# The first pass over a batch in two steps of groups instead of three, with two of its scores in the feed-forward's own banks and a pause behind each maximum and each exponential

## The chip, the cores and the metric

The kernel runs on one core of a Trainium2 chip. The metric is the device time of one execution in microseconds (us). Before the change it is 1489.42 us, the median of three runs (1488.94 to 1490.77).

## The reference

Two things are computed one after the other: an attention through 32 inducing points, and a feed-forward layer with a leaky ReLU over its result.

```
x: 4 batches x 12480 tokens x 128;  inducing: 32 x 128
def mab(q, kv):
    s = scale * (q @ kv.T);  s = s - s.max(-1);  a = exp(s);  a /= a.sum(-1) + 1e-9
    return a @ kv
h   = mab(inducing, x)          # per batch: 32 x 128, over all 12480 tokens
y   = mab(x, h)                 # per token, over 32 rows
out = max(0.01 * g, g) @ w_out, with g = y @ w_in      # 128 -> 2048 -> 128, for 49920 tokens
```

So every batch needs a first pass over all its tokens (scores against the inducing points, a maximum, exponentials, and products with the tokens' rows) before `h` is known, and only then the second softmax and the feed-forward work of that batch can begin.

## The kernel before

**Tiles and units.** A batch has 12480 tokens: six groups 0 to 5 of 2048 tokens and a rest group RG (number 6) of 192. The feed-forward work runs over tiles of 512 columns: four tiles per full group, and one tile of 384 columns for the rests of two batches together (the pair tile). There are 98 tiles, and each takes 16 units (one for each 128 of the 2048 hidden columns): 1568 units, numbered u = 16 x tile + f. One unit is four matmuls on TensorE: `ph` (L718, hidden values into one of three PSUM banks), and three `po` (L757: high and low part of the hidden values with high and low part of w_out). ScalarE makes the high part `ghi` from `ph` (L731), VectorE the low part `glo` (L739). TensorE runs three units ahead with `ph` (LOOK = 3): `ph` of unit u+3 is issued, then the three `po` of unit u. Behind the last unit of a tile stands one more product (L776, with `m2s`), which adds the linear part.

**Where the batches stand.** Batch 0 is prepared by a list written out by hand (ORDER). Its tiles 0 to 23 are units 0 to 383. Batch 1 begins with tiles 24 to 27 (its group 0), then comes tile 28, the pair tile of the rests of batches 0 and 1 (units 448 to 463), then group 1 from tile 29. Tile 77 is the pair tile of batches 2 and 3.

**What is woven in.** The loop over units (L1316 to L1341) issues one unit, and after it lets generators make one step each: `stores`, `stacking`, `fetches`, `seconds`, `scores`, `values`. A step that returns HEAVY (15) puts a debt on the loop that is paid off with 4 per unit (5 in batch 0); while there is debt, nothing but `stacking` and `fetches` makes a step. So the order on every engine is written by this loop, and each engine works through its own order.

- `first_scores` (L362) turns a batch's tokens (L397, VectorE) and takes the first pass in the steps of PASSES (L129): [RG, 0, 1], [2, 3], [4, 5]. A step's scores (`s1_ps`, L264, with `indT`) go to TensorE in one stretch, with up to two second scores of the batch before (`s2_ps`, L264, with `hT`) that were waiting, and with the value products of the step before (`h_ps`, L440). `peaks` (L269) takes the maxima on VectorE, `running` (L294) the running maximum and the exponentials.
- `first_values` (L462) turns the exponentials and adds the value products up (`hacc`). Then `expand_weights` (L533) makes the weights `hws` of that batch.
- `second` (L577) makes one group's second softmax and its turned result: `aT` for a full group, `aTr` for the rest group (L623). The groups come in the order 0, 1, RG, 2, 3, 4, 5 (L1341).
- `stack` (L628) splits that into `ahi` (L645, ScalarE) and `alo` (L650, GpSimd), and copies the pieces into the tile `A4` by DMAs on SyncE's queue (L664): four DMAs for a full tile, and 24 for a pair tile (two batches, three pieces, four rows of partitions), because its pieces are 32 partitions x 64 columns.
- `load_rows` (L216) fetches token rows `xr` by DMA on the same queue, `load_blocks` (L243) the blocks `xc` to be turned, `store` (L781) writes results: four DMAs of `osb` per tile.

`ph` of a tile's first unit waits for the DMAs of its `A4`.

Of the kernel before, what the change touches and what calls it, by code (L numbers as in the profile page):

```python
# [20 lines left out]
def induced_attention_then_leaky_ffn(  # L21
# [106 lines left out]
    ring = set()  # L128
    PASSES = [[RG, 0, 1], [2, 3], [4, 5]]  # L129
    PASS_OF = {g: p for p, gs in enumerate(PASSES) for g in gs}  # L130
# [71 lines left out]
    def room(n=1):  # L202

        return not rows_live or rows_made[0] + n - 1 - min(i for i, _ in rows_live) < XR

# [63 lines left out]
    def peaks(b, p, sps):  # L269

        gs = PASSES[p]
        rm = sb.tile([P, len(gs)], F32, tag="rm", name="rm", bufs=2)
        if RG in gs:
            nc.vector.memset(rm[:, :1], -3.0e38)
        for i, g in enumerate(gs):
            _, J, K = GROUPS[g]
            w, rows = 32 * K, 32 * J
            if g == RG:
                e = sb.tile([P, w], F32, tag="er", name="er", bufs=1)
            else:  # L280
                e = sb.tile([P, TOK], F32, tag="e", name="e", bufs=2)
            nc.vector.tensor_scalar(  # L282
                out=e[:rows, :w],
                in0=sps[g][:rows, :w],
                scalar1=1.0,
                scalar2=None,
                op0=ALU.mult,
                op1=ALU.max,
                accum_out=rm[:rows, i : i + 1],
            )  # L290
            ex[b, g] = e
        return rm

    def running(b, p, rm):  # L294
        gs = PASSES[p]
        n = len(gs)
        nm_old = maxima.get(b)
        zg = sb.tile([P, 3], F32, tag="zg", name="zg", bufs=2)
# [3 lines left out]
        four = sb.tile([M, 12], F32, tag="rd", name="four", bufs=2)  # L302
        al = None
# [3 lines left out]
        if nm_old is None:  # L307
            nc.vector.tensor_reduce(out=nm[:M], in_=four[:, : 4 * n], op=ALU.min, axis=AX.X)
        else:
            least = sb.tile([M, 12], F32, tag="least", name="least", bufs=2)  # L310
# [12 lines left out]
        for i, g in enumerate(gs):  # L323
            _, J, K = GROUPS[g]
            w, rows = 32 * K, 32 * J
            e = ex[b, g]
            nc.scalar.activation(  # L327
                e[:rows, :w], e[:rows, :w], AF.Exp, bias=nm[:rows], scale=SCALE,
                accum_out=zg[:rows, i : i + 1],
            )  # L330
            yield
        zs = sb.tile([P, 1], F32, tag="zs", name="zs", bufs=2)
# [29 lines left out]
    def first_scores(b):  # L362


        halves = [(RG, 0, 3)] + [(g, j0, 2) for g in range(RG) for j0 in (0, 2)]
        blocks = {}
# [9 lines left out]
        for p, gs in enumerate(PASSES):  # L376
# [24 lines left out]
            while p and not ((b, p - 1) in ready and landed(b, p - 1)):  # L401
                yield
            while b - 1 not in hw or hw[b - 1][2] is None or not room(min(2, len(waiting))):
# [16 lines left out]
            rm = peaks(b, p, sps)  # L420
            yield HEAVY
# [40 lines left out]
    def first_values(b):  # L462

        hacc = None
        for p, gs in enumerate(PASSES):
            while (b, p) not in summed:
                yield
            for g in gs:
# [5 lines left out]
                else:  # L474
                    ay = sb.tile([P, 16, M], F32, tag="ay", name="ay", bufs=2)
                nc.vector.transpose(ay[:rows, :K, :].rearrange("p k m -> p (k m)"), e[:rows, : 32 * K])
# [30 lines left out]
    def normalise(b, hacc, rz):  # L507

        same = e128.rearrange("p j m -> p (j m)")
        hs = sb.tile([P, C], F32, tag="hs", name="hs", bufs=1)  # L510
        nc.scalar.mul(hs, hacc, rz)
# [21 lines left out]
    def expand_weights(b):  # L533
# [4 lines left out]
        if b:  # L538
            while not room(2):
# [37 lines left out]
    def second(b, g, engines=None):  # L577
# [4 lines left out]
        rows, w = 32 * J, 32 * K  # L582
        if b == B - 1 and (b, g) not in early and g != RG and g > 1:
            while hw[b][2] is None or not room(len(waiting)):
# [257 lines left out]
    def start(stacking, seconds, chosen):  # L842
# [57 lines left out]
        def peak(g):  # L900
# [5 lines left out]
            if g == RG:  # L906
                e = sb.tile([P, TOK], F32, tag="e", name="e", bufs=2)
            else:
                e = sb.tile([P, TOK], F32, tag="A4", name="e0", bufs=A4_BUFS)
# [61 lines left out]
        def Y(g):  # L971
            J, K, rows, w = size(g)
            V["ay", g] = ay = sb.tile([P, 16, M], F32, tag="ay", name="ay", bufs=2)
            nc.vector.transpose(
# [35 lines left out]
        def gather(p):  # L1010
            hp = V.pop(("hp", p))[:, :C]
            if p == len(STEPS) - 1:
                V["hs"] = new = sb.tile([P, C], F32, tag="hs", name="hs", bufs=1)
                nc.vector.scalar_tensor_tensor(
# [20 lines left out]
        def scaled():  # L1035
            V["samez"] = r = sb.tile([P, P], F32, tag="samez", name="samez", bufs=1)
            nc.scalar.mul(r, same, V["rz"])
# [76 lines left out]
        def first_second():  # L1114
# [3 lines left out]
            yield  # L1118
            y = sb.tile([P, 16, M], F32, tag="y", name="y", bufs=1)
            chosen["ysub"].tensor_tensor(  # L1120
# [23 lines left out]
        def scales():  # L1144
            apart = sb.tile([P, 4, 16], F32, tag="apart", name="apart", bufs=1)
            nc.vector.tensor_tensor(
# [10 lines left out]
        def scales_copy():  # L1157
            r = sb.tile([P, 4, 16], F32, tag="scr", name="scr", bufs=1)
            nc.scalar.copy(r.rearrange("p t k -> p (t k)"), V.pop("sc")[:, :64])
# [46 lines left out]
        def second_turned(g):  # L1206
# [3 lines left out]
            if g:  # L1210
                y = sb.tile([P, 16, M], F32, tag="y", name="y", bufs=1)
                nc.vector.transpose(y.rearrange("p k m -> p (k m)"), V.pop(("s2", g)))
# [90 lines left out]
    with tc.manual_schedule():  # L1303
# [12 lines left out]
        for u in range(WOVEN, NT * NF):  # L1316
# [12 lines left out]
            if u >= 52 and u % 2:  # L1329
                step(fetches)  # L1330
            if not debt[0]:
                step(seconds)
            if u >= max(due[0], 52) and not debt[0]:
                due[0] = u + (2 if b or u % 4 else 1)
                step(scores)
            if u >= 52 and (u >= due[1] or hw[max(hw)][2] is None) and not debt[0]:
                due[1] = u + (2 if b or u % 4 else 1)
                known = len(hw)
                step(values)
                if len(hw) > known:  # L1340
                    seconds += [second(known, g) for g in [0, 1, RG, 2, 3, 4, 5]]  # L1341
        for gen in stores:
# [35 lines left out]
```

## Time and profile before

| | |
|---|---|
| median of three runs | 1489.42 us |
| the profiled execution: its time, and the span of its instructions | 1489.34 us, 1487.1 us |
| TensorE (PE) busy | 1477.0 us, 99% |
| VectorE (DVE) busy | 1262.5 us, 85% |
| ScalarE (ACT) busy | 998.8 us, 67% |
| GpSimd (POOL) busy | 116.5 us, 8% |
| share of PE in the chain that ended last | 97% |

Busy time is the time in which at least one instruction of the engine runs. The profiled execution took 2.24 us more than its span: what lies ahead of the first and behind the last instruction. SPq is SyncE's queue of DMA issues; an issue there has a duration of its own, and the data lands later.

### The profile page before, as it was taken

Reading aid. Unit: us, or ns where it says so; the run is one execution under the profiler, and the core shown is the slowest. Engines: PE = TensorE matmul, PEld = TensorE weight load, DVE = VectorE, ACT = ScalarE, POOL = GpSimd, SP = SyncE. Lnnn points to the kernel's source line nnn. Section 1 sums busy time; section 2 is a strip of 40 time slices with the busy share of each in tenths; the row PEclk is TensorE's granted clock in tenths of the full one; section 3 lists DMA queues with packets and bytes.
Section 4 is the critical chain, followed back from the end, with each engine's and each line's share of the span. In section 5 each row is a group of like instructions: output and inputs, shape, how many; then the busy total and the mean of one; then the engine's idle time right before and its main releaser. Section 6 shows DMA issues by size and latency. Waiting matters only on the chain.

```text
span 1487.1 us, 22254 instructions
## 1 busy us (share of the span) xinstructions
PE 1477.0 (99%) x7861; PEld 1260.3 (85%) x7861; DVE 1262.5 (85%) x2129; ACT 998.8 (67%) x1749; POOL 116.5 (8%) x186
## 2 busy tenths in 40 slices
PE   8999999999999999999999999999999999999998
PEld 6788888888888888888888888888888898888887
DVE  6889889889898898889898898788888888888886
ACT  6766767666665766667665766676776666666665
POOL 1320100000100100000100100010100000000000
PEclk9999999999999999999999999999999999999999
DMA  8336255444444342343443441231212212212211
GB/s 287 68 80 124 47 94 113 94 91 77 88 91 89 89 90 52 57 87 70 89 86 69 109 92 17 49 71 21 45 37 39 44 21 51 43 22 50 41 24 22
DMA packets 402079, 105.23 MB, mean 71 GB/s; under 512 B 372624, under 2 KB 375088, under 8 KB 401968
## 3 DMA queue, kind: packets, MB, share of 16 engines
q1 hardware_dynamic: 401920, 103.80, 34.5%
q8 instruction: 62, 1.02, 0.3%
q14 instruction: 49, 0.40, 0.1%
q10 hardware_dynamic: 48, 0.02, 0.0%
HBM read 48.94 MB, written 25.56 MB: 50 GB/s over the span
## 4 chain that ended last, share of the span: by engine, by line
PE 97%; DMA 1%; SPq 0%; ACT 0%; DVE 0%; issue 0%; DVEq 0%
PE po L757 68%; PE ph L718 23%; PE s_ps L264 3%; PE po L776 1%; DMA xr<-in_x_dram 1%; PE h_ps L440 1%; PE h_ps L1001 0%; SPq L852 0%; PE hw_ps L547 0%; PE w_ps L1101 0%; PE winT_ps L1091 0%; ACT ghi L731 0%; PE a_ps L1182 0%; DVE osb L786 0%; ACT e L327 0%
## 5 line engine op out<-in xcount | busy, mean ns | idle before, releaser
L731 ACT ACTIVATE ghi<-ph 128x512 fp32r<-128x512 f32 (+1 forms) x1568 | 928.4, 595 | 460.1 <-PE ph L718 454.0
L739 DVE SCALAR_TENSOR_TENSOR glo<-ph,ghi 128x512 fp32r<-128x512 f32 (+1 forms) x1568 | 1042.9, 680 | 183.3 <-ACT ghi L731 161.6
L718 PE MATMUL ph<-A,hws 128*128 128x512 f32 (+1 forms) x1600 | 595.0, 377 | 0.4 <-ACT A L1186 0.3
L757 PE MATMUL po<-glo,w_hi 128*128 128x512 f32 (+1 forms) x1568 | 593.0, 378 | 0.0
L757 PE MATMUL po<-ghi,w_lo 128*128 128x512 f32 (+1 forms) x1568 | 593.0, 378 | 0.0
L757 PE MATMUL po<-ghi,w_hi 128*128 128x512 f32 (+1 forms) x1568 | 592.8, 379 | 0.0
L718 PEld LDWEIGHTS ph<-A,hws 128*128 128x128 f32 x1600 | 301.8, 189 | 58.1 <-DVE e L282 5.0
L757 PEld LDWEIGHTS po<-glo,w_hi 128*128 128x128 f32 x1568 | 296.4, 189 | 41.2
L757 PEld LDWEIGHTS po<-ghi,w_lo 128*128 128x128 f32 x1568 | 296.3, 189 | 41.2
L757 PEld LDWEIGHTS po<-ghi,w_hi 128*128 128x128 f32 x1568 | 296.4, 189 | 39.9 <-ACT ghi L731 0.2
L786 DVE STREAM_TRANSPOSE osb<-po 128x512 f32<-128x512 f32 (+1 forms) x98 | 68.9, 703 | 1.5 <-PE po L776 1.5
L650 POOL TENSOR_TENSOR alo<-aT,ahi 128x512 fp32r<-128x512 f32 x22 | 28.2, 1282 | 516.9 <-ACT ahi L645 479.7
L397 DVE STREAM_TRANSPOSE xT<-xc 128x512 f32<-128x512 f32 x72 | 50.5, 701 | 0.0
L599 POOL TENSOR_TENSOR y<-y,mx 128x512 f32<-128x512 f32 x23 | 24.2, 1050 | 228.9 <-DVE mx L597 194.5
L614 POOL TENSOR_TENSOR y<-y,sm 128x512 f32<-128x512 f32 x23 | 24.2, 1050 | 199.8 <-DVE sm L612 168.9
L776 PE MATMUL po<-A,m2s 128*128 128x512 f32 (+1 forms) x100 | 37.1, 374 | 0.0
L357 DVE STREAM_TRANSPOSE y<-s_ps 128x512 f32<-128x512 f32 x22 | 15.8, 716 | 10.9 <-PE s_ps L264 9.3
L264 PE MATMUL s_ps<-xT,hT 128*32 128x512 f32 x192 | 23.8, 596 | 0.4 <-ACT hT L1045 0.4
L264 PE MATMUL s_ps<-xT,indT 128*32 128x512 f32 x192 | 24.0, 594 | 0.0
L776 PEld LDWEIGHTS po<-A,m2s 128*128 128x128 f32 x100 | 18.9, 189 | 2.6
L282 DVE TENSOR_SCALAR_CACHE_REDUCE e<-s_ps 128x512 f32<-128x512 f32 x18 | 12.4, 690 | 8.0 <-PE s_ps L264 7.3
L440 PEld LDWEIGHTS h_ps<-xr,ay 128*32 128x32 f32 x576 | 15.2, 110 | 2.9 <-issue 2.6
(165 smaller groups left out, 375.1 us busy)
## 6 DMA issues: line engine op xcount, KB each, us to landing
xr<-in_x_dram SPq DMA_DIRECT2D x96, 256.0 KB, 4.4
out_dram<-osb SPq DMA_DIRECT2D x384, 64.0 KB, 2.2
xc<-in_x_dram SPq DMA_DIRECT2D x288, 64.0 KB, 2.7
A<-ahi SPq DMA_DIRECT2D x188, 64.0 KB, 2.0
A<-alo SPq DMA_DIRECT2D x188, 64.0 KB, 2.0
hws<-hilo SPq DMA_DIRECT2D x64, 64.0 KB, 2.0
raw<-in_moe_w_in_dram SPq DMA_DIRECT2D x4, 512.0 KB, 7.3
raw<-in_moe_w_out_dram SPq DMA_DIRECT2D x4, 512.0 KB, 9.4
```

Of the source, the lines that this page charges most:

```text
L264: nc.tensor.matmul(dst, lhsT, rhs, start=True, stop=True)
L397: nc.vector.transpose(t[:, j, :], blk.rearrange("p n c -> p (n c)"))
L440: nc.tensor.matmul(hp[32 * k : 32 * k + 32, :C], ay[:rows, 4 * q + k, :], xb[:rows, k, :], start=(i == 0 and q == 0), stop=(last[k] == i a ...
L599: engines[0].tensor_tensor(out=yv, in0=yv, in1=mx[:rows, :K].unsqueeze(2).broadcast_to([rows, K, M]), op=ALU.subtract,)
L614: engines[1].tensor_tensor(out=yv, in0=yv, in1=smv.unsqueeze(2).broadcast_to([rows, K, M]), op=ALU.mult)
L650: (engine or nc.gpsimd).tensor_tensor(out=alo[sl], in0=aT.pop((b, g))[: 32 * J, :], in1=ahi[sl].bitcast(F32), op=ALU.subtract,)
L718: nc.tensor.matmul(ph[:, o : o + w], hw[b][1][:, f * P : (f + 1) * P], woven(A4[t][:, o : o + w], t), start=True, stop=True,)
L731: nc.scalar.activation(halves(ghi[:, :n], t)[1], live[u][2], AF.Relu)
L739: nc.vector.scalar_tensor_tensor(out=halves(glo[:, :n], t)[1], in0=ph, scalar=0.0, in1=halves(ghi[:, :n], t)[1].bitcast(F32), op0=ALU.max, ...
L757: nc.tensor.matmul(accs[t][:, :n], w[:, f, :], woven(r[:, :n], t), start=(f == 0 and w is w_hi and r is live[u][0]), stop=False,)
L776: nc.tensor.matmul(accs[t][:, o : o + w], hw[b][2], woven(a4[:, o : o + w], t), start=False, stop=(o + w == n),)
L786: nc.vector.transpose(osb[:, :n], po[:, :n])
```

## The change

The first pass has two steps, [0, 1, 2] and [RG, 5, 3, 4], instead of three. In the first step all waiting second scores (three of them now, groups 3 to 5; groups RG, 2, 0 and 1 are taken in `expand_weights`) go into the three `ph` banks, and the step's own three scores into the two auxiliary banks and the `hp` bank. In the second step RG and 5 go into `ph` banks. Behind each maximum but the last of a step and behind each exponential stands HEAVY. Tokens' rows are taken when a slot is free, not when the oldest is. In the loop `seconds` and `scores` are stepped in that order as before, `values` comes first only while a batch's weights are not finished, and a debt made by one ends the others' turn. Some tiles share a tag (and so a buffer) to make room for a third `e` and a third `ay`.

```
-    PASSES = [[RG, 0, 1], [2, 3], [4, 5]]
+    PASSES = [[0, 1, 2], [RG, 5, 3, 4]]
...
-        return not rows_live or rows_made[0] + n - 1 - min(i for i, _ in rows_live) < XR
+        return len(rows_live) + n <= XR
...
-                e = sb.tile([P, TOK], F32, tag="e", name="e", bufs=2)
+                e = sb.tile([P, TOK], F32, tag="e", name="e", bufs=3)
...
             ex[b, g] = e
+            if i + 1 < len(gs) and g != RG:
+                yield HEAVY
...
                 accum_out=zg[:rows, i : i + 1],
             )
-            yield
+            yield HEAVY
...
-        halves = [(RG, 0, 3)] + [(g, j0, 2) for g in range(RG) for j0 in (0, 2)]
+        halves = [h for gs in PASSES for g in gs for h in ([(RG, 0, 3)] if g == RG else [(g, 0, 2), (g, 2, 2)])]
...
-            for q in [waiting.pop(0) for _ in range(min(2, len(waiting)))]:
+            for q in [waiting.pop(0) for _ in range(len(waiting))]:
...
-                if g == RG:
+                if g == 2:
                     sps[g] = ps_s.tile([P, TOK], F32, tag="hp", name="s1_ps")
+                elif g in (RG, 5):
+                    sps[g] = gen_ps("s1_ps")
                 else:
                     sps[g] = aux_ps("s1_ps")
...
-            for g, ps in [(RG, gen_ps("s2_ps")), (0, aux_ps("s2_ps")), (1, ps_s.tile([P, TOK], F32, tag="hp", name="s2_ps"))]:
+            for g in (RG, 2, 0, 1):
+                if g == 1:
+                    ps = ps_s.tile([P, TOK], F32, tag="hp", name="s2_ps")
+                else:
+                    ps = aux_ps("s2_ps") if g == 0 else gen_ps("s2_ps")
                 second_scores(b, g, ps)
                 turned(b, g, ps)
-            waiting.extend(range(2, RG))
+            waiting.extend(range(3, RG))
...
-            if not debt[0]:
-                step(seconds)
-            if u >= max(due[0], 52) and not debt[0]:
-                due[0] = u + (2 if b or u % 4 else 1)
-                step(scores)
-            if u >= 52 and (u >= due[1] or hw[max(hw)][2] is None) and not debt[0]:
...
+            urgent = hw[max(hw)][2] is None
+            for lane in (values, seconds, scores) if urgent else (seconds, scores, values):
+                if debt[0]:
+                    break
+                if lane is seconds:
+                    step(seconds)
+                elif lane is scores:
+                    if u >= max(due[0], 52):
+                        due[0] = u + (2 if b or u % 4 else 1)
+                        step(scores)
+                elif u >= 52 and (u >= due[1] or urgent):
...
```

**Place one: VectorE, from the first score stretch of batch 2 to the turned rest group `aTr` of batch 1.** Before; `y<-s_ps` are the second scores, `e,rm<-s_ps` the maxima, and each `glo` is one unit:

```order
L357 STREAM_TRANSPOSE y<-s_ps 128x512 x2
L274 MEMSET rm 128x1
L282 TENSOR_SCALAR er,rm<-s_ps 96x64
L282 TENSOR_SCALAR e,rm<-s_ps 128x512 x2
L739 SCALAR_TENSOR_TENSOR glo<-ph,ghi 128x512 x3
L300 MEMSET zg 128x1
L739 SCALAR_TENSOR_TENSOR glo<-ph,ghi 128x512
L623 STREAM_TRANSPOSE aTr<-yr 96x64
```

There `aTr` stands four units behind the stretch. The same place of the kernel after the change, in two pieces that follow each other:

```order
L359 STREAM_TRANSPOSE y<-s_ps 128x512 x3
L282 TENSOR_SCALAR e,rm<-s_ps 128x512
L747 SCALAR_TENSOR_TENSOR glo<-ph,ghi 128x512 x4
L631 STREAM_TRANSPOSE aT<-y 128x512
L747 SCALAR_TENSOR_TENSOR glo<-ph,ghi 128x512 x4
L794 STREAM_TRANSPOSE osb<-po 128x512
L747 SCALAR_TENSOR_TENSOR glo<-ph,ghi 128x512 x4
L282 TENSOR_SCALAR e,rm<-s_ps 128x512
L747 SCALAR_TENSOR_TENSOR glo<-ph,ghi 128x512 x4
L605 TENSOR_REDUCE mx<-yr 96x2
L747 SCALAR_TENSOR_TENSOR glo<-ph,ghi 128x512 x4
L282 TENSOR_SCALAR e,rm<-s_ps 128x512
```

Then, behind it:

```order
L747 SCALAR_TENSOR_TENSOR glo<-ph,ghi 128x512 x4
L794 STREAM_TRANSPOSE osb<-po 128x512
L747 SCALAR_TENSOR_TENSOR glo<-ph,ghi 128x512 x6
L617 TENSOR_REDUCE sm<-yr 96x2
L310 TENSOR_REDUCE nm<-four 32x1
L747 SCALAR_TENSOR_TENSOR glo<-ph,ghi 128x512
L619 TENSOR_SCALAR sm<-sm 96x2
L620 RECIPROCAL sm<-sm 96x2
L747 SCALAR_TENSOR_TENSOR glo<-ph,ghi 128x512 x5
L794 STREAM_TRANSPOSE osb<-po 128x512
L747 SCALAR_TENSOR_TENSOR glo<-ph,ghi 128x512 x8
L631 STREAM_TRANSPOSE aTr<-yr 96x64
```

Here `aTr` stands 44 units behind the stretch (4 + 4 + 4 + 4 + 4 + 4 + 6 + 1 + 5 + 8), and the stretch itself stands behind 386 `glo` of the program instead of 362: `aTr` has moved from behind the 366th to behind the 430th unit.

**Place two: SyncE's queue, ahead of the pair tile's DMAs (`A<-ahi` and `A<-alo` of 32x64).** Before; the last row is the first of the 24:

```order
L664 DMA A_5094<-alo 32x512
L222 DMA xr<-in_x_dram 96x256
L222 DMA xr<-in_x_dram 128x512 x2
L810 DMA out_dram<-osb 256x2x32 x4
L664 DMA A_5336<-ahi 32x64
```

After:

```order
L250 DMA xc<-in_x_dram 32x16x32 x16
L818 DMA out_dram<-osb 256x2x32 x8
L222 DMA xr<-in_x_dram 128x512 x3
L818 DMA out_dram<-osb 256x2x32 x4
L222 DMA xr<-in_x_dram 128x512 x2
L672 DMA A_5859<-ahi 32x64
```

Three stores more stand ahead of them than before, that is, the 24 DMAs are issued three to four tiles later; they still stand ahead of those of tile 29.

**Place three: TensorE, a stretch of the first pass of batch 1 with its value products `h_ps`.** Before, the stretch of the second of three steps:

```order
L757 MATMUL po<-ghi,w_lo 128x512
L440 MATMUL h_ps<-xr,ay 32x128 x32
L440 MATMUL h_ps<-xr,ayr 32x128 x2
L264 MATMUL s_ps<-xT,hT 32x512 x4
L264 MATMUL s_ps<-xT,indT 32x512 x8
L718 MATMUL ph<-A_1955,hws 128x512
```

After, the stretch of the second of two:

```order
L765 MATMUL po<-ghi,w_lo 128x512
L444 MATMUL h_ps<-xr,ay 32x128 x48
L264 MATMUL s_ps<-xTr,indT 32x64 x3
L264 MATMUL s_ps<-xT,indT 32x512 x12
L726 MATMUL ph<-A_2701,hws 128x512
```

One stretch of each of the batches 1 to 3 is gone from TensorE's order, and its products stand in the others. The number of matmuls of every kind is the same in both programs.

## Rows read from the trace of the kernel before

**Rows 1.** The page, busy time of each engine, share of the span, instructions.
```profile
PE 1477.0 (99%) x7861; PEld 1260.3 (85%) x7861; DVE 1262.5 (85%) x2129; ACT 998.8 (67%) x1749; POOL 116.5 (8%) x186
```
**Rows 2.** Windows: stretch in us, busy us of PE, PEld, DVE, ACT, POOL; clock; DMA.
```profile
0.00:44.00 44.00, 39.93 (x452) 26.43 (x453) 30.20 (x91) 27.80 (x58) 8.11 (x12) 1.00 0.75 250
...
400.00:800.00 400.00, 400.00 (x2106) 343.61 (x2105) 348.99 (x591) 270.79 (x477) 29.30 (x51) 1.00 0.40 77
800.00:1487.00 687.00, 681.21 (x3404) 590.08 (x3402) 568.91 (x896) 461.48 (x791) 35.95 (x52) 1.00 0.23 46
```
**Rows 3.** Waits of PE: line, releaser, us in total, times, longest.
```profile
PE xT_ps L880 <- DMA xr<-in_x_dram: 1.5, 2, 1.0
```
**Rows 4.** Timeline of PE about one lone stretch of value products: start, duration, engine.
```profile
298.72 0.38 PE L757 MATMUL po<-ghi,w_lo 128*128 128x512 f32 x1
299.03 1.74 PE L440 MATMUL h_ps<-xr,ay 128*32 128x128 f32 x56
...
300.92 0.48 PE L718 MATMUL ph<-A,hws 128*128 128x512 f32 x1
301.24 0.38 PE L757 MATMUL po<-ghi,w_hi 128*128 128x512 f32 x1
```
**Rows 5.** Timeline of the first score stretch of batch 2.
```profile
382.72 1.92 PE L264 MATMUL s_ps<-xT,hT 128*32 128x512 f32 x16
382.81 0.69 DVE L739 SCALAR_TENSOR_TENSOR glo<-ph,ghi 128x512 fp32r<-128x512 f32 x1 [0.17 <-ACT ghi L731]
...
384.46 0.23 PE L264 MATMUL s_ps<-xTr,indT 128*32 128x64 f32 x3
...
387.55 0.69 DVE L739 SCALAR_TENSOR_TENSOR glo<-ph,ghi 128x512 fp32r<-128x512 f32 x1 [0.30 <-ACT ghi L731]
```
**Rows 6.** Timeline: the pair tile's pieces on VectorE, ScalarE, GpSimd.
```profile
390.74 0.23 DVE L623 STREAM_TRANSPOSE aTr<-yr 96x64 f32<-96x64 f32 x1
...
398.85 0.38 ACT L645 CAST ahi<-aTr 96x64 fp32r<-96x64 f32 x2
...
399.16 0.60 POOL L650 TENSOR_TENSOR alo<-aTr,ahi 96x64 fp32r<-96x64 f32 x2 [2.99 <-ACT ahi L645]
```
**Rows 7.** Timeline of SyncE's queue: the pair tile's 24 DMAs, the first and the last.
```profile
398.60 3.24 SPq L810 DMA_DIRECT2D out_dram<-osb  x4
401.95 0.56 SPq L664 DMA_DIRECT2D A<-ahi  x1
...
416.50 0.59 SPq L664 DMA_DIRECT2D A<-alo  x1
417.13 2.00 SPq L222 DMA_DIRECT2D xr<-in_x_dram  x4
```
**Rows 8.** DMA issues from 401.9 to 417.2 us: count, size, us to landing.
```profile
A<-alo SPq DMA_DIRECT2D x12, 8.0 KB, 1.7
```
**Rows 9.** Timeline at unit 430, and at unit 448, the pair tile's first.
```profile
446.30 0.38 PE L718 MATMUL ph<-A,hws 128*128 128x512 f32 x1
446.72 0.60 ACT L731 ACTIVATE ghi<-ph 128x512 fp32r<-128x512 f32 x1 [0.27 <-PE ph L718]
447.09 0.70 DVE L397 STREAM_TRANSPOSE xT<-xc 128x512 f32<-128x512 f32 x1
...
462.06 0.36 PE L718 MATMUL ph<-A,hws 128*128 128x192 f32 x2
```
**Rows 10.** PE by forms from 446.25 to 462.03 us: count, busy us, mean ns.
```profile
L718 PE MATMUL ph<-A,hws 128*128 128x512 f32 x18 | 6.8, 379 | 0.0
```
**Rows 11.** Timeline of tile 29's split and its first DMA.
```profile
450.66 0.61 ACT L645 CAST ahi<-aT 128x512 fp32r<-128x512 f32 x1
...
451.30 0.57 SPq L664 DMA_DIRECT2D A<-ahi  x1
```
**Rows 12.** PE by forms, 1.3 to 4.1 us and 4.1 to 7 us: busy, mean ns.
```profile
L1242 PE MATMUL warm_ps<-ident 128*128 128x256 bf16 x13 | 2.9, 416 | 1.4 <-POOL ident masks.py:199 1.4
...
L1242 PE MATMUL warm_ps<-ident 128*128 128x256 bf16 x20 | 2.8, 278 | 0.0
```

More of the change, by code (lines that the diff above doesn't have):

```diff
@@ L297, in running @@
         nm_old = maxima.get(b)
-        zg = sb.tile([P, 3], F32, tag="zg", name="zg", bufs=2)
+        zg = sb.tile([P, 4], F32, tag="zg", name="zg", bufs=2)
         if RG in gs:
@@ L301, in running @@
         nm = sb.tile([P, 1], F32, tag="nm", name="nm", bufs=3)
-        four = sb.tile([M, 12], F32, tag="rd", name="four", bufs=2)
+        four = sb.tile([M, 16], F32, tag="rd", name="four", bufs=2)
         al = None
@@ L309, in running @@
         else:
-            least = sb.tile([M, 12], F32, tag="least", name="least", bufs=2)
+            least = sb.tile([M, 16], F32, tag="least", name="least", bufs=2)
             nc.vector.tensor_scalar(
@@ L402, in first_scores @@
                 yield
-            while b - 1 not in hw or hw[b - 1][2] is None or not room(min(2, len(waiting))):
+            while b - 1 not in hw or hw[b - 1][2] is None or not room(len(waiting)):
                 yield
@@ L419, in first_scores @@
             visited.add((b, p))
-            rm = peaks(b, p, sps)
+            rm = yield from peaks(b, p, sps)
             yield HEAVY
@@ L474, in first_values @@
                 else:
-                    ay = sb.tile([P, 16, M], F32, tag="ay", name="ay", bufs=2)
+                    ay = sb.tile([P, 16, M], F32, tag="ay", name="ay", bufs=3)
                 nc.vector.transpose(ay[:rows, :K, :].rearrange("p k m -> p (k m)"), e[:rows, : 32 * K])
@@ L509, in normalise @@
         same = e128.rearrange("p j m -> p (j m)")
-        hs = sb.tile([P, C], F32, tag="hs", name="hs", bufs=1)
+        hs = sb.tile([P, C], F32, tag="hacc", name="hs", bufs=2)
         nc.scalar.mul(hs, hacc, rz)
@@ L538, in expand_weights @@
         if b:
-            while not room(2):
+            while not room(3):
                 yield
-            for g, ps in [(RG, gen_ps("s2_ps")), (0, aux_ps("s2_ps")), (1, ps_s.tile([P, TOK], F32, tag="hp", name="s2_ps"))]:
+            for g in (RG, 2, 0, 1):
[3 more added lines that the diff above has]
+                    ps = aux_ps("s2_ps") if g == 0 else gen_ps("s2_ps")
                 second_scores(b, g, ps)
                 turned(b, g, ps)
-            waiting.extend(range(2, RG))
+            waiting.extend(range(3, RG))
         pw = aux_ps("hw_ps")
@@ L582, in second @@
         rows, w = 32 * J, 32 * K
-        if b == B - 1 and (b, g) not in early and g != RG and g > 1:
+        if b == B - 1 and (b, g) not in early and g != RG and g > 2:
             while hw[b][2] is None or not room(len(waiting)):
@@ L906, in peak @@
             if g == RG:
-                e = sb.tile([P, TOK], F32, tag="e", name="e", bufs=2)
+                e = sb.tile([P, TOK], F32, tag="e", name="e", bufs=3)
             else:
@@ L972, in Y @@
             J, K, rows, w = size(g)
-            V["ay", g] = ay = sb.tile([P, 16, M], F32, tag="ay", name="ay", bufs=2)
+            V["ay", g] = ay = sb.tile([P, 16, M], F32, tag="ay", name="ay", bufs=3)
             nc.vector.transpose(
@@ L1012, in gather @@
             if p == len(STEPS) - 1:
-                V["hs"] = new = sb.tile([P, C], F32, tag="hs", name="hs", bufs=1)
+                V["hs"] = new = sb.tile([P, C], F32, tag="hacc", name="hs", bufs=2)
                 nc.vector.scalar_tensor_tensor(
@@ L1035, in scaled @@
         def scaled():
-            V["samez"] = r = sb.tile([P, P], F32, tag="samez", name="samez", bufs=1)
+            V["samez"] = r = sb.tile([P, P], F32, tag="m2s", name="samez", bufs=2)
             nc.scalar.mul(r, same, V["rz"])
@@ L1118, in first_second @@
             yield
-            y = sb.tile([P, 16, M], F32, tag="y", name="y", bufs=1)
+            y = sb.tile([P, 16, M], F32, tag="e", name="y", bufs=3)
             chosen["ysub"].tensor_tensor(
@@ L1144, in scales @@
         def scales():
-            apart = sb.tile([P, 4, 16], F32, tag="apart", name="apart", bufs=1)
+            apart = sb.tile([P, 4, 16], F32, tag="er", name="apart", bufs=1)
             nc.vector.tensor_tensor(
@@ L1157, in scales_copy @@
         def scales_copy():
-            r = sb.tile([P, 4, 16], F32, tag="scr", name="scr", bufs=1)
+            r = sb.tile([P, 4, 16], F32, tag="ayr", name="scr", bufs=1)
             nc.scalar.copy(r.rearrange("p t k -> p (t k)"), V.pop("sc")[:, :64])
@@ L1210, in second_turned @@
             if g:
-                y = sb.tile([P, 16, M], F32, tag="y", name="y", bufs=1)
+                y = sb.tile([P, 16, M], F32, tag="e", name="y", bufs=3)
                 nc.vector.transpose(y.rearrange("p k m -> p (k m)"), V.pop(("s2", g)))
@@ L1330, in induced_attention_then_leaky_ffn @@
                 step(fetches)
-            if not debt[0]:
-                step(seconds)
-            if u >= max(due[0], 52) and not debt[0]:
-                due[0] = u + (2 if b or u % 4 else 1)
-                step(scores)
-            if u >= 52 and (u >= due[1] or hw[max(hw)][2] is None) and not debt[0]:
[L1337 to L1341, printed above, removed]
+            urgent = hw[max(hw)][2] is None
[9 more added lines that the diff above has]
+                elif u >= 52 and (u >= due[1] or urgent):
+                    due[1] = u + (2 if b or u % 4 else 1)
+                    known = len(hw)
+                    step(values)
+                    if len(hw) > known:
+                        seconds += [second(known, g) for g in [0, 1, RG, 2, 3, 4, 5]]
         for gen in stores:
```

## The prediction

> **What bounds the kernel now.** I read the shares of busy time first: TensorE is busy for 1477.0 of 1487.1 us [rows 1]. Then the windows, to see where the other 10 us are: 4.1 us in the first 44 us, 5.8 us behind 800 us (the end, where the last result is stored), and none from 400 to 800 us [rows 2]. Then TensorE's waits: the largest is for the first rows of x, 1.5 us in all [rows 3], at the start, which the change leaves as it is. So from 44 us on TensorE does one matmul behind the other, and the question for every part of the change is only whether TensorE gets less to do, or is made to wait. What VectorE, ScalarE and GpSimd are spared costs or gains nothing as long as TensorE finds its operands ready. The last thing to read is therefore how far ahead of its use each operand is made; there the order of the changed program and the trace of before have to be put together.
>
> **The change part by part.**
>
> *Stretches.* The first pass of batches 1 to 3 has one stretch less on TensorE each, with the same matmuls in all. A stretch costs something beyond its products, where TensorE goes from the feed-forward's matmuls to others and back. At the lone stretch of value products the last `po` starts at 298.72 and the stretch at 299.03, 0.31 us later; behind it `ph` starts at 300.92 and the next `po` at 301.24, 0.32 us later [rows 4]. Within the feed-forward work 18 units and one product take 446.30 to 462.06 us [rows 9, 10], 73 matmuls in 15.76 us, 0.216 us each. So a stretch costs 0.09 + 0.10 = 0.2 us, and three stretches less give 0.6 us back. This is the only gain on the path that I find.
>
> *Small instructions.* A step less per batch takes away three sets of small ones on VectorE, ScalarE and GpSimd (the running maximum, the factor `al`, one addition to `hacc`). TensorE's solid work hides them: nothing.
>
> *Longer stretches.* The first step now issues three second scores and three first ones at a time, six score groups; before it were four and the small RG. Two groups take 382.72 to 384.46, 0.87 us each [rows 5], so the stretch grows from 3.7 to some 5.2 us. The third score needs the third `ph` bank, which `glo` of the newest unit frees: 382.81 + 0.69 = 383.50, and the third group would begin at 384.46 [rows 5], so it is free by then with 0.96 us to spare. In the stretch VectorE has three transposes and a maximum, about 0.7 us each like its other 128x512 instructions, 2.8 us in all, shorter than the stretch. Queued behind them is `glo` of the next unit; TensorE needs it only after three units of 0.86 us that it has ready, and in the stretch of before, with 2.9 us of such work, `glo` came at 387.55 [rows 5] and no wait stands in the list. I take 0; if VectorE were late by one such instruction in each of the three stretches, 2.1 us. The pauses behind maxima and exponentials move VectorE's work apart, and the added third buffers for `e` and `ay` cover the longer time that these live.
>
> *What the pauses push back.* With HEAVY behind each maximum and exponential the loop is in debt for longer, and `seconds`, which waits for the same debt, falls back. Most tiles don't feel it: their DMAs are issued at the same unit in both programs, held back by the six `A4` buffers. The pair tile of batches 0 and 1 does. Its piece `aTr` of batch 1 comes behind `glo` of the 366th unit of the program before and of the 430th after (place one), while its first matmul stays at unit 448. Before, the split was followed by 24 DMAs which nobody waited for. After, the chain is this. In the trace of before, the transpose that stands in the same place, behind `glo` of the 430th unit, starts at 447.09 [rows 9]; `aTr` takes 0.23 us [rows 6], to 447.32. `ahi` stands behind `ghi` of unit 430, which ends at 446.72 + 0.60 = 447.32 [rows 9], so it goes on at once; its two halves take 0.38 us [rows 6], the first 0.19. A DMA that waits for `ahi` starts 0.03 us behind it (450.66 + 0.61, then 451.30) [rows 11]. So the first of the 24 starts at about 447.55. From the first to the last start the 24 took 401.95 to 416.50 us, 14.55 us [rows 7], since SyncE's queue issues one in 0.63 us; the last lands 1.7 us after its issue [rows 8]. That is 447.55 + 14.55 + 1.7 = 463.8. TensorE has 18 units between [rows 10] and would begin the tile's second half at 462.06 + 0.09 = 462.15 [rows 9]. It waits for **1.7 us**.
>
> The bounds of this term: if the DMAs went at the pace of the four row loads behind them (2.00 us for four, 0.5 each [rows 7]), the last would start 11.5 us after the first and land at 460.8, before TensorE needs it: 0. If four stores stood in the way as in the trace of before, where `alo` ended at 399.76 [rows 6] and the first DMA started at 401.95 [rows 7], 2.2 us later, counted from `alo`'s end after the change (about 448.3), the last would land at 466.7: 4.6 us. I take 1.7, because the DMAs are the same ones and the stores that stand ahead of them now are made by about unit 425. Queued behind the 24 on SyncE are three row loads, a store, two row loads and then the four DMAs of tile 29; by the same rows (0.5 each for loads, 3.2 for four stores, 0.63 for pieces) its four land about 447.55 + 15.1 + 2.5 + 3.2 + 2.5 + 1.7 = 472.6, and the tile begins 16 units of 0.86 us behind the pair tile, at 475.9 or later: no second wait.
>
> *The sum.* 1489.34 (the profiled execution's own time, which is the median of the three runs within 0.1 us) - 0.6 + 1.7 = **1490.4 us**, 0.07% above.
>
> **The rivals.**
>
> 1. *The pair tile is in time.* For it: the bound of 0 above; against it: both ends of the chain come from rows of the same instructions. Then only the stretches count: 1489.34 - 0.6 = 1488.7.
>
> 2. *Slower: SyncE's queue is late when the pair tile's pieces are ready.* In the new order stores of three tiles stand ahead of the 24 (place two). A store waits for its `osb`, and if the last of them is still being issued, the wait grows from the point at which the queue comes free later than 447.6; at the delay of before it is 4.6 us, and the time 1489.34 - 0.6 + 4.6 = 1493.3. Against it: the last store's transpose stands eight units ahead of `aTr`.
>
> 3. *Slower: VectorE is late behind the longer stretches.* This decides if `glo` of the unit behind a stretch ends over three units after TensorE resumes. With 2.1 us for three, and the pair tile's wait, 1492.5. Against it: VectorE's own 85% [rows 1], and no such wait in before.
>
> 4. *The clock.* TensorE starts at the lower of its two levels (1.2 and 2.4 GHz): 13 warming matmuls from 1.4 to 4.1 us have a mean of 416 ns, the next 20 one of 278 [rows 12]. If the wait at the pair tile brought the lower level back for as long, 2.7 us at up to half speed, it costs up to 1.4 us more: 1491.8. Against it: windows with short waits stand at 1.00 [rows 2, 3]. The Trainium skill (TensorE: Matmul & The Clock Gate, "What's actually happening") says that the lower clock is the default and that only activity keeps TensorE out of it; that would make any wait on a solid TensorE dearer than itself. The trace agrees for the start alone; no run here shows a fall from a wait in the middle.
>
> 5. *Faster by more than the stretches.* It would have to come from time that TensorE loses now, and there is none between 44 us and the end that the rows show. It is open only if merged stretches cost much less than I see.
>
> **How the numbers follow.** The forecast (a wait of 1 to 3 us at the pair tile) gets 0.57, rival 1 0.15, rival 2 0.11, rival 3 0.07, rival 4 0.05, rival 5 0.05. What a measurement of this kernel can tell from no change is about 0.2%, 3.0 us: 1486.4 to 1492.4. The forecast, rival 1, and rival 4 lie inside (0.77, of which I give 0.01 to slower), rivals 2 and 3 above it (0.18), rival 5 below (0.05): faster 0.05, same 0.76, slower 0.19. The range reaches from rival 1 with the spread of the runs (about 0.4 us down) to rival 2: 1488.3 to 1493.4. It leaves out rival 5 and what lies above 1493.4, together less than 2 in 10.
>
> **What would show it.** Right: in the list of waits TensorE has one line for `ph` released by a DMA of `A`, once, 1 to 3 us, at about 462 us; the last of the 24 DMAs lands at that moment; no other wait on TensorE behind 44 us; the rest of TensorE's busy time is the same within 1 us. Wrong: no such line (rival 1), the first of the 24 starting over 1 us after `ahi` (rival 2), waits of `po` for VectorE behind the stretches at about 159, 407 and 772 us (rival 3), or a granted clock below 1.00 behind 462 us (rival 4). A time below 1486 or above 1494 us would say that I have missed something on TensorE.

## The result, and the profile after

The changed kernel takes 1503.37 us (median of five runs, 1501.85 to 1503.86) against 1489.42 before: a ratio of 1.009 [1.0079, 1.01], 0.9% slower. I had forecast 1490.4 and a range that ended at 1493.4, so the prediction was wrong. The profiled execution took 1501.85 us with a span of 1500.1, 13.0 us more than before. The kernel before was run again beside each of the experiments below (medians 1489.59 to 1490.08), and each ratio is to those runs. Runs in a slow state, one of them (1933.59 us) of the kernel with half the pieces by GpSimd, are left out of all figures.

The page, and the windows of the stretches that matter (columns as in [rows 2]), of the kernel after:

```profile
PE 1480.7 (99%) x7861; PEld 1262.5 (84%) x7861; DVE 1258.2 (84%) x2114; ACT 998.8 (67%) x1746; POOL 112.6 (8%) x165
```

```profile
89.00:400.00 311.00, 304.13 (x1627) 257.48 (x1626) 264.92 (x452) 202.02 (x354) 24.67 (x41) 0.99 0.44 83
333.61:336.10 2.49, 0.00 (x0) 0.00 (x0) 0.00 (x0) 0.00 (x0) 0.00 (x0) 1.00 0.52 82
336.10:343.00 6.90, 3.85 (x47) 3.12 (x48) 0.00 (x0) 0.32 (x1) 0.00 (x0) 0.51 0.50 87
343.00:476.10 133.10, 130.06 (x647) 107.52 (x645) 114.16 (x193) 86.18 (x153) 9.66 (x20) 1.00 0.34 62
476.10:479.50 3.40, 3.40 (x10) 2.85 (x11) 1.19 (x4) 1.49 (x3) 0.08 (x1) 0.50 0.94 261
479.50:1490.00 1010.50, 1010.46 (x5175) 873.89 (x5174) 857.11 (x1390) 685.34 (x1184) 62.61 (x89) 1.00 0.30 58
```

TensorE is still busy for 99%, and busy for 3.7 us longer than in [rows 1] with the same 7861 matmuls: part of its work ran at a lower clock. The windows say where. Between 89 and 400 us it stands still for 6.9 us, between 343 and 476 us for 3.0, and with each of these standstills comes a stretch with a granted clock of 0.50 (1.2 of 2.4 GHz), 6.8 and 3.4 us long. The first of them begins while TensorE still stands: 2.5 us after its last matmul, with 3.0 us to go until the next. So TensorE works for only 3.85 of those 6.8 us. The second begins as the wait ends, and TensorE works through all of it. Behind 479.5 us, up to 1490, no wait and no lower clock is left.

The waits of TensorE (columns as in [rows 3]):

```profile
PE h_ps L444 <- DMA xr<-in_x_dram: 6.9, 2, 5.5
PE ph L726 <- DMA A<-alo: 3.0, 1, 3.0
```

The second is the wait that I forecast, in its place. The first and larger one I did not have at all: value products of batch 1's second step, `h_ps`, wait for the tokens' rows. No wait of `po` or `ph` for VectorE stands in the list.

The timeline of TensorE (columns as in [rows 4]) shows that stretch, and behind the "..." the same stretch of batch 2, where nothing is late:

```profile
330.33 1.52 PE L444 MATMUL h_ps<-xr,ay 128*32 128x128 f32 x48
333.18 0.43 PE L444 MATMUL h_ps<-xr,ay 128*32 128x128 f32 x8 [1.33 <-DMA xr<-in_x_dram]
339.15 2.36 PE L444 MATMUL h_ps<-xr,ay 128*32 128x128 f32 x40 [5.54 <-DMA xr<-in_x_dram]
341.28 0.64 PE L444 MATMUL h_ps<-xr,ayr 96*32 96x128 f32 x4
341.86 0.79 PE L726 MATMUL ph<-A,hws 128*128 128x512 f32 x1
...
343.36 0.38 PE L726 MATMUL ph<-A,hws 128*128 128x512 f32 x1
...
665.20 2.83 PE L444 MATMUL h_ps<-xr,ay 128*32 128x128 f32 x96
...
668.16 0.48 PE L726 MATMUL ph<-A,hws 128*128 128x512 f32 x1
```

From its first product to the next `ph` the stretch takes 341.86 - 330.33 = 11.53 us, in batch 2 it takes 2.96: 8.6 us more, and 0.5 more in the unit behind it, which still runs at the lower clock. Of these 9.1 us 6.9 are the two waits. Of the 2.2 that remain the lower clock accounts for 1.9, half of the 3.85 us that TensorE worked at 0.50.

Why the rows are late stands in SyncE's queue (start, duration, count of DMA issues):

```profile
303.84 0.56 SPq L222 DMA_DIRECT2D xr<-in_x_dram  x1
304.45 16.24 SPq L250 DMA_DIRECT2D xc<-in_x_dram  x24
320.79 1.03 SPq L222 DMA_DIRECT2D xr<-in_x_dram  x2
...
329.52 0.58 SPq L222 DMA_DIRECT2D xr<-in_x_dram  x1
...
332.71 2.67 SPq L818 DMA_DIRECT2D out_dram<-osb  x4
335.42 0.62 SPq L222 DMA_DIRECT2D xr<-in_x_dram  x1
```

The program asks for the 13 loads of rows that this step needs one by one, and for the last four of them only after it has asked for the first blocks of batch 2: 24 DMAs that the queue issues in 16.24 us, 0.68 each. Between the four loads stand 16 DMAs of pieces for `A4` and a store. So the load of 329.52 is used at 333.18, and the last, issued from 335.42 to 336.04, is what the product at 339.15 waits for, 3.1 us later. In the program before, the last rows that the step needs stand ahead of those blocks:

```profile
277.39 1.15 SPq L222 DMA_DIRECT2D xr<-in_x_dram  x1
...
291.70 19.27 SPq L250 DMA_DIRECT2D xc<-in_x_dram  x28
```

The pair tile, its pieces and its first matmuls, in the timeline after:

```profile
457.84 0.23 DVE L631 STREAM_TRANSPOSE aTr<-yr 96x64 f32<-96x64 f32 x1
457.96 0.39 ACT L653 CAST ahi<-aTr 96x64 fp32r<-96x64 f32 x2
458.21 0.58 SPq L672 DMA_DIRECT2D A<-ahi  x1
...
460.77 1.56 SPq L672 DMA_DIRECT2D A<-ahi  x1
...
472.80 0.25 PE L726 MATMUL ph<-A,hws 128*128 128x192 f32 x1
...
474.21 0.59 SPq L672 DMA_DIRECT2D A<-alo  x1
...
476.10 0.50 PE L726 MATMUL ph<-A,hws 128*128 128x192 f32 x1 [3.04 <-DMA A<-alo]
...
476.87 0.63 PE L765 MATMUL po<-glo,w_hi 128*128 128x512 f32 x1
477.30 0.63 PE L765 MATMUL po<-ghi,w_lo 128*128 128x512 f32 x1
477.73 0.58 PE L726 MATMUL ph<-A,hws 128*128 128x192 f32 x2
...
479.43 0.41 PE L726 MATMUL ph<-A,hws 128*128 128x192 f32 x2
```

The chain is the forecast one, 10.7 us later than in the forecast (472.80 against 462.06 for the tile's first `ph`): 9.1 us are the loss before it, and the rest is work of the longer stretches that now stands ahead of this tile. The 24 DMAs start from 458.21 to 474.21: 16.0 us, where [rows 7] had 14.55; one issue alone took 1.56. The second half starts 3.30 us behind the first, where 0.09 would do, and from there to the next unit's `ph` and on to the one after it take 1.63 and 1.70 us, where 0.78 and 0.87 would do: 3.2 + 1.7 = 4.9 us. The 1.7 is again half of the 3.40 us at 0.50.

So 9.1 + 4.9 = 14.0 us are lost in two places, and the span grew by 13.0. The starts of `ph`, unit by unit, put 1.2 us of gain into the stretches that are fewer now. The 0.2 us that remain are rounding and small differences that nearly cancel: the first unit starts 0.4 us earlier, and at a few units more than before `ph` slips by 0.1 to 0.25 us, in all 0.4.

### The profile page after: what moved, and what is told of

Same layout as the page of the kernel before. It is cut to its first block, busy times and chain, and to the rows that moved or that the text cites. A ratio compares the mean times of both kernels' runs of the same rounds, so it can differ in the third digit from the quotient of the medians.

```text
span 1500.1 us, 22215 instructions
## 1 busy us (share of the span) xinstructions
PE 1480.7 (99%) x7861; PEld 1262.5 (84%) x7861; DVE 1258.2 (84%) x2114; ACT 998.8 (67%) x1746; POOL 112.6 (8%) x165
## 4 chain that ended last, share of the span: by engine, by line
PE 97%; SPq 1%; DMA 1%; DVE 0%; issue 0%; ACT 0%; DVEq 0%; ACTq 0%
PE po L765 67%; PE ph L726 23%; PE s_ps L264 3%; PE po L784 1%; PE h_ps L444 1%; SPq L672 1%; DMA xr<-in_x_dram 1%; PE xT_ps L888 1%; PE hw_ps L555 0%; PE w_ps L1109 0%; SPq L818 0%; DVE ay L982 0%; PE winT_ps L1099 0%; DMA A<-alo 0%; SPq L860 0%
## 5 line engine op out<-in xcount | busy, mean ns | idle before, releaser
L444 PE MATMUL h_ps<-xr,ay 128*32 128x128 f32 x576 | 18.4, 284 | 6.9 <-DMA xr<-in_x_dram 6.9
L359 DVE STREAM_TRANSPOSE y<-s_ps 128x512 f32<-128x512 f32 x22 | 15.7, 716 | 4.2 <-PE s_ps L264 2.2
```

What stands on the lines that cost most here:

```text
L444: nc.tensor.matmul(hp[32 * k : 32 * k + 32, :C], ay[:rows, 4 * q + k, :], xb[:rows, k, :], start=(i == 0 and q == 0), stop=(last[k] == i a ...
```

## The experiments

Two theories stood against each other. Mine after the trace: two late transfers on SyncE's queue, each of which also brings the lower clock, are the whole loss, and each can be removed by its position in the queue alone. The rival: the longer stretches and the pauses cost something themselves, and what is late is only where it shows.

**The blocks of the next batch behind the last rows.** In `first_scores`, ahead of the first three blocks, with `issued` filled in `load_rows`:

```
+        issued.add((b, g, q))
...
+        while b > 1 and (b - 1, 4, 3) not in issued:
+            yield
         for _ in range(3):
             more()
```

> The changed kernel, but the first three block loads of a batch (24 DMAs of SyncE's queue, 16.2 us) are issued only when the last rows of the batch before have been issued. Late-rows theory: in the changed kernel TensorE's value products of batch 1 wait 6.9 us for rows that stood behind those 24 issues, and the lower clock afterwards costs some 2.3 us more; both go: 1503.4 - 9.2 = 1494.2 us, with the pair tile's wait of 3.0 us still there. Rival (the rows are late because their loads begin late and come one in four units, whatever stands ahead): the wait stays over 1 us and the time above 1502. Rival (longer stretches and pauses hold VectorE up): no change from 1503.

Measured: 1494.17 us (1492.4 to 1497.6), ratio 1.0028 [1.0016, 1.0039]. In its queue the last load of rows now stands ahead of the blocks:

```profile
320.41 0.62 SPq L223 DMA_DIRECT2D xr<-in_x_dram  x1
321.07 16.39 SPq L252 DMA_DIRECT2D xc<-in_x_dram  x24
```

and of the two long waits only the pair tile's is left:

```profile
PE ph L730 <- DMA A<-alo: 3.4, 1, 3.4
```

The time is the one expected, and the queue's order was the cause of the first loss.

**The rest group second.** Its turned piece `aTr` comes one group earlier:

```
-                        seconds += [second(known, g) for g in [0, 1, RG, 2, 3, 4, 5]]
+                        seconds += [second(known, g) for g in [0, RG, 1, 2, 3, 4, 5]]
```

> The changed kernel, but the second softmax takes the rest group right behind group 0 instead of behind group 1, which brings the pair tile's DMAs forward by 40 units. Late-DMA theory: the pair tile's wait (3.0 us and 1.9 us at the lower clock behind it) goes, the wait for rows stays: 1503.4 - 4.9 = 1498.5 us. Rival (TensorE's 13 us come from the longer stretches and the pauses, and the waits only show where it would have waited anyway): less than 2 us gained.

Measured: 1497.54 us (1496.69 to 1499.13), ratio 1.0053 [1.004, 1.0066], a microsecond under the expected time. The pair tile's wait is gone, that for the rows is still there, 0.6 us longer:

```profile
PE h_ps L444 <- DMA xr<-in_x_dram: 7.5, 2, 5.6
```

**Both.** The two edits together.

> Both edits: blocks behind rows, and the rest group second. Late-DMA theory: neither wait is left, the clock stays at its higher level from the start to the end, and the three stretches less that the prediction counted show: 1489.4 - 0.6 to - 1.1, so 1488.3 to 1488.8 us. Rival (something else in the change costs time too): 1490 or more.

Measured: 1487.84 us (1486.95 to 1490.39, eleven runs), ratio 0.9987 [0.9978, 0.9996]: faster than the kernel after, a little faster than the one before, and 0.5 us below the range that I gave. Its largest wait, and its windows from 89 to 800 us:

```profile
PE warm_ps L1254 <- POOL ident masks.py:199: 1.4, 1, 1.4
```

```profile
89.00:400.00 311.00, 311.00 (x1669) 264.60 (x1668) 273.49 (x468) 208.07 (x365) 24.21 (x42) 1.00 0.45 85
400.00:800.00 400.00, 399.96 (x2130) 341.10 (x2129) 344.20 (x578) 266.06 (x465) 29.01 (x52) 1.00 0.38 74
```

That wait stands ahead of the first matmul of all. In the windows TensorE stands still no more, and its clock is the higher one throughout. With two steps and all pauses in place nothing of the loss is left: the rival falls, as far as the sum goes.

**The rows awaited in the program.** Instead of the queue's order, the other end of the same wait. `LAND` is the number of units that the loop puts between the last load of a step's rows and the products with them; here with the rest group second:

```
-    LAND = 12
+    LAND = 24
```

> The changed kernel with the rest group second (e2), the block loads where the change has them, and a margin of 24 units instead of 12 between the last row load and the value products. Late-rows theory: the products of batch 1 go to TensorE's order ten units later, where the rows have landed or nearly so; the wait of 6.9 us goes or shrinks below 1 us, and the time is 1488 to 1489 us. Rival (the queue only slips with it, since the loads behind it are issued from the same loop): the wait stays over 3 us, and the time above 1492.

Measured: 1489.35 us (1487.98 to 1490.63), ratio 0.9998 [0.9989, 1.0007], a little over the range that I gave. No wait of the products for rows stands in its list. So 12 units (10 us) are too few when 16.24 us of blocks, pieces and a store stand ahead in the queue, and holding the products back mends it too. It stays 1.5 us above the kernel with both edits, though the intervals of the two ratios overlap. Of the 1.9 us between the two profiled executions 1.2 lie ahead of the first `ph`, where this edit changes nothing, and 0.7 in small slips of `ph` behind it.

**No pauses.** The changed kernel with a plain `yield` behind maxima and exponentials:

```
-                yield HEAVY
+                yield
...
-            yield HEAVY
+            yield
```

> The changed kernel without the pauses: where a maximum or an exponential of the first pass returned HEAVY, it returns nothing, the rest of the change stays. Late-DMA theory: the pauses are what pushed the pieces back; without them rows and pair tile are ready in time and the time is that of both edits, 1488.3 to 1490 us. Rival (the pauses protect VectorE: without them glo comes late behind the score stretches): waits of po or ph for VectorE appear, and the time is 1491 or more although no DMA is late.

Measured: 1490.62 us (1489.63 to 1492.43), ratio 1.0004 [0.9996, 1.0013], between the two forecasts: 0.6 us above my range and 0.4 below the rival's. Neither the rows nor the pair tile's pieces are late. Two small waits for VectorE are there:

```profile
PE ph L726 <- DVE glo L747: 0.7, 2, 0.5
```

The profiled executions of this kernel and the one with both edits lie 3.8 us apart: 1.3 of it ahead of the first `ph`, and 2.6 behind it, where `ph` slips by 0.1 to 0.65 us at more units (the line above names 0.7 of it). So the rival is right in a small part: the pauses do something, but they save lateness of VectorE rather than cost time.

The rows are in time here although six of their 13 loads still stand behind the 24 block loads. The pieces for `A4` come after the loads now, and the last load is issued well ahead of the products:

```profile
305.45 1.46 SPq L222 DMA_DIRECT2D xr<-in_x_dram  x1
...
317.47 2.83 PE L444 MATMUL h_ps<-xr,ay 128*32 128x128 f32 x96
```

**Only the pauses.** The kernel before, its three steps kept, with the pauses alone:

```
-            rm = peaks(b, p, sps)
+            rm = yield from peaks(b, p, sps)
...
+                yield HEAVY
```

> The kernel before, with its three steps of groups, and only the pauses of the change: HEAVY behind each maximum but the last of a step and behind each exponential. The pair tile's DMAs are then issued 49 units ahead of their use (72 before, 17 in the changed kernel), and the last rows of batch 1 stand ahead of the next batch's block loads by 37 units. Late-DMA theory: neither is late, no wait on TensorE, the same 22 stretches as before: 1489 to 1490 us. Rival (the pauses by themselves cost the time, wherever the passes end): over 1495 us.

Measured: 1489.52 us (1488.64 to 1491.31), ratio 0.9998 [0.9989, 1.0007]. Its one larger line of waits is at the start, as in [rows 3], where the rows of x come late to the first transposes:

```profile
PE xT_ps L882 <- DMA xr<-in_x_dram: 2.6, 3, 1.5
```

In this profiled execution two of them, close to each other, brought the lower clock too. The last row is a window behind them:

```profile
9.46 0.66 PE L882 MATMUL xT_ps<-ident,xr 128*128 128x128 f32 x4 [1.50 <-DMA xr<-in_x_dram]
10.43 0.63 PE L882 MATMUL xT_ps<-ident,xr 128*128 128x128 f32 x4 [0.32 <-DMA xr<-in_x_dram]
...
11.00:14.20 3.20, 3.20 (x16) 1.54 (x16) 0.19 (x1) 0.00 (x0) 0.00 (x0) 0.50 1.01 363
```

Neither the pauses nor the two steps lose anything clear of the runs' spread alone. Together they do: of these kernels only the changed one issues the last load of rows after TensorE has come to the products (335.42 against 330.33 us), and has `aTr` behind unit 430 (397 without the pauses, 398 with the pauses alone).

**The clock: the wait filled.** The other three runs ask what the lower clock depends on. They start from the first experiment, whose one wait is 3.4 us. Here 28 small products without use stand between the halves of the pair tile's first `ph`:

```
+            if u == 28 * NF and b == 1:
+                bits, pw = ident.bitcast(BF16), aux_ps("fill_ps")
+                for _ in range(28):
+                    nc.tensor.matmul(pw[:, : 2 * P], bits[:, :P], bits, start=True, stop=True)
```

> The kernel with the blocks behind the rows (e1), and between the two matmuls of the pair tile's first unit TensorE does 28 small matmuls of 256 columns into a spare bank, about 3.1 us of work at the higher level, in place of most of its wait of 3.4 us. They do nothing for the output. If the lower clock behind the wait (6.8 us in e1, 2.9 us lost by time) comes from the idle stretch: no stretch below 1.00 behind it, and the time is 1494.2 - 2.9 = 1491.3 us. Rival (the clock falls for another reason, the DMA burst or the matmuls of 192 columns): the clock falls as before, and the time stays at 1494.

Measured: 1492.09 us (1490.87 to 1493.09), ratio 1.0017 [1.0007, 1.0026], 0.8 us above what I gave. First, from the first experiment, the window behind the unfilled wait, and then its first matmuls there:

```profile
467.50:474.30 6.80, 6.19 (x18) 5.31 (x19) 2.35 (x5) 2.08 (x5) 1.27 (x1) 0.50 0.81 197
```

```profile
468.11 0.50 PE L730 MATMUL ph<-A,hws 128*128 128x192 f32 x1 [3.42 <-DMA A<-alo]
468.41 0.68 PE L769 MATMUL po<-ghi,w_hi 128*128 128x512 f32 x1
```

The same place with the wait filled:

```profile
465.00 3.23 PE L733 MATMUL fill_ps<-ident 128*128 128x256 bf16 x28
467.98 0.34 PE L734 MATMUL ph<-A,hws 128*128 128x192 f32 x1
468.16 0.40 PE L773 MATMUL po<-ghi,w_hi 128*128 128x512 f32 x1
```

TensorE gets nothing useful done in the 3.0 us from 464.90 to 467.98, but behind them a `po` takes 0.40 us and not 0.68, and the granted clock stays at 1.00. The pieces are as late as before: the last was issued at 466.04 us here and at 466.23 in the first experiment. It is TensorE's standing still, not the lateness, that brings the lower level.

**The clock: half the pieces by GpSimd.** In `stack`:

```
-                        nc.sync.dma_start(
+                        queue = nc.gpsimd if t == 28 and r % 2 else nc.sync
+                        queue.dma_start(
```

> The kernel with the blocks behind the rows (e1), but 12 of the pair tile's 24 DMAs are issued by GpSimd, whose engine is 8% busy, and 12 by SyncE. Issue theory: the wait is the time in which one queue issues 24 DMAs (16 us); with half of them on each queue the last lands some 7 us earlier, before TensorE comes to the tile: no wait, the clock stays, and the time is that of both edits, 1487.8 us. Rival (what is late is the split, or the landing of so many small pieces): a wait of over 1 us stays.

Measured: 1488.62 us (1487.9 to 1489.19, ten runs), ratio 0.9994 [0.9985, 1.0004], 0.8 us above what I gave. The pair tile's wait is gone, as with `aTr` earlier: it was the one queue's issue time that was too long.

**The clock: a shorter wait.** Three of the 24 by GpSimd (`r == 3 and b == 1` in the line above).

> As e7, but with only three of the 24 DMAs on GpSimd's queue, to shorten the wait by 1.9 us to some 1.5 us. By the prediction's rival on the clock as the runs have it so far (waits of 3.0 and 3.4 us were followed by 3.4 and 6.8 us at half clock, waits of 1.4 us at the start by none): a wait of 1.5 us leaves the clock at 1.00, and the time is 1487.8 + 1.5 = 1489.3 us. Rival (any wait on a solid TensorE lowers the clock): a stretch at 0.50 follows, and the time is 1491 or more.

Measured: 1490.19 us (1489.06 to 1490.84), ratio 1.0004 [0.9995, 1.0013], 0.9 us above what I gave and below the rival's 1491. The wait, and the window around it:

```profile
PE ph L731 <- DMA A<-ahi: 1.4, 1, 1.4
```

```profile
464.00:470.00 6.00, 4.64 (x27) 4.02 (x26) 3.62 (x8) 3.22 (x9) 1.07 (x1) 1.00 0.61 162
```

A wait of 1.4 us in the same place leaves the clock at 1.00 and costs little more than itself: 1490.19 - 1488.62 = 1.6 us against the kernel with half the pieces by GpSimd, run at the same time.

## Why the prediction was wrong

**The step that failed** is a sentence of "What the pauses push back": "Most tiles don't feel it: their DMAs are issued at the same unit in both programs, held back by the six `A4` buffers." I looked at what the pauses do to `A4`'s pieces, which `stack` brings, and did not look at the tokens' rows, which go through the same queue and have their own consumer. Four loads of rows now stand behind 24 block loads, and the last of them behind 16 pieces and a store as well; what those cost the queue, and who waits for the rows, are what the sum lacks. It is 9.1 of the 14.0 us lost. "No other wait on TensorE behind 44 us" followed from the same gap. The moved loads stand in the order of SyncE's queue at the rows of batch 1; the two pieces that I took of it (place two) are both from the pair tile, where I already expected something.

**The pair tile.** The mechanism was right, the size was not: 1.7 us forecast, 3.0 measured, inside the bounds of 0 to 4.6. The term that was too small is the time of the 24 issues, which I took from [rows 7]: 14.55 us against 16.0, and 16.4 and 15.7 in two of the experiments. Each of these three has one issue of 1.23 to 1.74 us among them, which [rows 7] had not; why, the runs don't show. The rest of the chain held within 0.2 us.

**Rival 4, the clock,** came true, twice, and I had priced it too low: at most 1.4 us; it cost 1.9 us behind the rows and, of the 4.9 at the pair tile, 1.7. In the first experiment it is 1494.17 - 1487.84 - 3.4 = 2.9 us for one wait of 3.4 (half of the 6.19 us of work at 0.50 is 3.1). My ground against it ("windows with short waits stand at 1.00") held for short waits only: the longest of [rows 3] is 1.0 us. The clock's column could not have shown the start either: it gives 1.00 for the first 44 us [rows 2], and only the matmuls' durations [rows 12] show the lower level there. I had read the start's length [rows 12] as a bound for a fall in the middle, and nothing in those rows makes it one. The Trainium skill (TensorE: Matmul & The Clock Gate, "What's actually happening") has the lower level as the default that only activity keeps away; the prediction found that borne out for the start alone. Now runs show it in the middle: 3.0 to 3.4 us of standing still brought it in two kernels, and the filled wait did not. Nor does every wait bring it: behind 1.4 us alone the clock stayed at 1.00, so the prediction's "any wait" went too far.

**Rivals 2 and 3** did not come: SyncE's queue was free 2.8 us ahead of the first of the 24, and no `po` or `ph` in the list of waits is held by VectorE, so the longer stretches cost nothing that stands in it, as forecast (0, bound 2.1); the slips of `ph`, 0.4 us more than before, do not stand behind them.

**The stretches** gave 1.2 us, not 0.6. That is 0.4 us for each stretch less rather than the 0.2 that I worked out from the way in and out of one [rows 4]. The kernel with both edits shows what the change is worth without the late loads: 1487.84 us, near rival 1's 1488.7.

So what the change does beside its transfers was forecast within a microsecond, and the 13 us came from where it puts them. The sum to 1490.4 lacked 9.1 us of the rows, 1.5 (3.2 - 1.7) and 1.7 of the pair tile, and had 0.6 too little gain: 1490.4 + 9.1 + 3.2 - 0.6 = 1502.1, where the profiled execution took 1501.85.

## What to carry to other kernels

When a change moves steps, follow every DMA that those steps issue, by kind, to the queue it stands in, and ask of each who waits for it and what is now ahead of it; a distance counted in units of the program says nothing about the queue's own pace (0.5 to 0.7 us for one issue here, of 8 KB as of 256 KB). Where TensorE is solid, a wait of some three microseconds may cost nearly twice its length (3.4 + 2.9 us here), and the price to add is half of the work done at the lower clock. A wait of 1.4 us alone cost about itself, but 1.50 and 0.32 us close together at the start of one run did bring the lower clock. And where a loss is a matter of place in a queue, two lines that put the urgent loads first can give it all back.

## What the runs showed of the hardware

- TensorE's granted clock fell to 0.50 while or just after TensorE stood still: at 336.1 us, 2.5 us into a wait of 5.5 (6.8 us at 0.50, 3.0 of them still in the wait); in the first experiment 2.8 us into a wait of 3.4 (6.8 us, 0.6 of them in the wait); at the pair tile as a wait of 3.0 ended (3.4 us, all of it work).
- One wait of 1.4 us in the middle left the clock at 1.00. Two of 1.50 and 0.32 us, 0.65 us of work between them, were followed by 3.4 us at 0.50 (only the pauses, 10.9 to 14.3 us). So the length of the longest wait alone does not decide it in these runs.
- At 0.50 a `po` of 512 columns starts 0.43 us behind the one before (476.87 to 477.30); at 1.00 it is 0.22.
- From the first start to the last the same 24 DMAs of 8 KB took 14.55 us in the kernel before and 16.0 in the one after on SyncE's queue, where one issue took 1.56 us and the others mostly 0.59. With half of them on GpSimd's queue an issue there took 0.50 us and landed 2.4 us later, on SyncE's 2.0:

```profile
A<-ahi SPq DMA_DIRECT2D x12, 8.0 KB, 2.0
A<-alo POOLq DMA_DIRECT2D x12, 8.0 KB, 2.4
```
